# A linear-attention block in front of two MLPs on one core: the stretch ahead of the first MLP step rebuilt, and the first steps and attention levels put in another order

## The chip, the core and the metric

The kernel runs on one core of a Trainium2 chip. Five engines work side by side: TensorE multiplies matrices into PSUM (PE in the profile, its weight loads PEld), VectorE (DVE), ScalarE (ACT) and GpSimd (POOL) work on tiles, and SyncE (SP) issues most DMAs. Each engine takes its instructions in the order in which they are written; they wait for each other on semaphores. The metric is device time in microseconds of one launch.

## What is computed

The attention runs over 24 chunks of 32 tokens for 4 batches and 8 heads; its output, as 3072 tokens of 256 values, goes through a squared-relu MLP and then through a second MLP with a clipped gate. Cut to its core:

```python
for c in range(nc):
    cum = np.cumsum(la, axis=-1)                       # la: log of the decays of this chunk
    L = np.exp(cum[:, :, :, None] - cum[:, :, None, :]) * causal
    y_intra = np.einsum('bhij,bhjd->bhid', np.einsum('bhin,bhjn->bhij', Cc, Bc) * L, xc)
    y_inter = np.einsum('bhin,bhnd->bhid', Cc, state) * np.exp(cum)[:, :, :, None]
    y[:, :, sl] = y_intra + y_inter
    Bx = np.einsum('bhjn,bhjd->bhjnd', Bc, xc) * np.exp(cum[:, :, -1:] - cum)[:, :, :, None, None]
    state = np.exp(np.sum(la, axis=-1))[:, :, None, None] * state + np.sum(Bx, axis=2)

x = x.transpose(0, 2, 1, 3).reshape(3072, 256)
h = np.maximum(x @ w_in, 0.0);  x = (h * h) @ w_out    # first MLP, 256 -> 2048 -> 256
h = x @ w2_in;  y = (h * np.clip(h + 3.0, 0.0, 6.0) / 6.0) @ w2_out
```

## The kernel before

**Attention by levels.** The kernel takes chunks of 64 tokens (`CH`); the same chunk of all four batches is one *level*, so there are 12 levels, 0 to 11. Two levels make a tile of 512 tokens for the MLP: tile t needs levels 2t and 2t+1. For a level, `load`, `load_ef` and `load_x` bring B, C, the decays and x; `scale` multiplies the decays `ef` into B and C (tile `bc`), `heads` writes C masked by head (`cb`), `tokens` multiplies decays into the token-wise B (in tile `xb`), `scores` multiplies B by masked C on TensorE, `mask` copies the causal part to `mt`, `inter`, `intra` and `update` are the three products of the level, `advance` makes the next state S, and `evac_h` (ACT) and `evac_l` (DVE) split the output into a high and a low part (`act_h`, `act_l`).

**The decays.** `products` scans the decays of all chunks on 96 rows; `decays` makes the scaled products and inverses (`efr`) on DVE for four chunks, two at a time; `spread` brings them by TensorE to the 128 rows of levels 0 and 1, `f_tokens` transposes them for `tokens`; levels 2 to 11 read them back from DRAM (`scr`), which `decays_out` writes.

**The first MLP by steps.** A step (t, f) takes one tile t and one block f of 128 of the 2048 hidden columns. `mm1` makes six matmuls of 512 columns (`ha`), `gate` is relu and square on ACT (or the square on DVE) and a split of the result into `gha` (ACT) and `gla` (DVE), and `mm2` makes six matmuls (`ya`) for the step two before it (`LAG` 2). There are 96 steps. The list `ORDER` says in which order they come: ten blocks of tile 0, ten of tile 1, the last six of tile 0, the last six of tile 1, then tile after tile. The sum of a tile that is interrupted is kept in `part`.

**The weights.** The first MLP's weights come in 16 pieces j of 512 KB (even j for `mm1`, odd for `mm2`; pieces 2q and 2q+1 serve blocks 2q and 2q+1). Each is loaded raw (`dma`), converted on ACT (`early`), rebuilt on DVE by three instructions (`join`: `sign`, `bits`, `merge`) and split into `ah` on ACT and `al` on POOL (`split`). `JOIN1` and `DMA1` say at which step a piece is joined and loaded.

**What sets the order.** There is no scheduler: the order in the program is the order on each engine. `PLAN` says which attention work is put at which step; from level 2 on a level takes four steps. In a step, attention work of TensorE (`state`: `inter` and `update`; `chunk`: `intra` and the next level's `scores`) comes behind `mm1`; the rest comes in `mid`, behind the gate, and `advance` there comes last, behind the `join`. A new step's split of a weight is made by `ready`, between the relu and the square. `keep_busy` issues bf16 matmuls on zeros that fill TensorE's idle time ahead of the first step. SP's DMAs rotate over eight semaphores; the ninth is issued when the first has landed. Pools of PSUM: `ps_s` (tile `big`, later `yu`) and `ps_a` (tile `att`, one buffer) have four banks each; a new `att` tile waits for the last reader of the old one.

## Time and profile before

| | us |
|---|---|
| median of 3 runs | 582.83 (581.58 to 583.52) |
| the profiled execution, its own time | 582.18 |
| span of the profiled execution | 580.5 |
| TensorE busy | 559.0 (96%) |
| DVE, ACT, POOL busy | 414.6, 362.3, 143.6 |
| first `ha` matmul of the first step starts | 22.34 |

In the profile, times are counted from the span's start. A row of the timeline has the start, the duration, the engine, the line, the operation with its output and inputs, the number of instructions that the row merges, and in brackets the idle time of the engine before it with what ended it. Durations of merged rows are those of the whole stretch. The float32 matmuls of the attention stand twice in the trace for each one in the program. 1.68 us of the profiled execution's time lie outside its span.

### The profile page before, as it was taken

What the parts mean: (1) busy time and instruction counts of PE and PEld (TensorE: products, weight loads), DVE (VectorE), ACT (ScalarE), POOL (GpSimd) and SP (SyncE); (2) the same over time, 40 slices, a digit from 0 to 9 for tenths busy, and PEclk for the clock granted to TensorE, in tenths of its full rate; (3) what the DMA queues carried; (4) which work ended last, traced back from release to release, by engine and by line L of the source; (5) the groups of instructions that cost most, each with busy time, mean ns of one, the idle gap of its engine ahead of it and who ended that gap; (6) DMA issues with size and microseconds to landing.
All of it is one profiled execution on the core that took longest, in us unless ns stands there. A gap on an engine that the chain in (4) does not pass through costs nothing.

```text
span 580.5 us, 10441 instructions
## 1 busy us (share of the span) xinstructions
PE 559.0 (96%) x4144; PEld 446.8 (77%) x4144; DVE 414.6 (71%) x658; ACT 362.3 (62%) x632; POOL 143.6 (25%) x196
## 2 busy tenths in 40 slices
PE   7799989999999999999999899999999999999996
PEld 3476667777778888888887688888788888788885
DVE  5797577766655676676776876887767978676774
ACT  4577675544444656665665776777766777666663
POOL 4465334420000244434258300330000600000000
PEclk9789999999999999999999999999999999999999
DMA  8895244213000212212210000000200000200002
GB/s 246 224 259 137 63 125 132 81 51 102 2 1 0 72 41 71 70 43 69 74 40 34 1 1 0 1 1 1 73 1 0 1 1 1 73 1 0 1 0 73
DMA packets 26464, 31.42 MB, mean 54 GB/s; under 512 B 2128, under 2 KB 21040, under 8 KB 26416
## 3 DMA queue, kind: packets, MB, share of 16 engines
q1 hardware_dynamic: 24544, 29.85, 18.2%
q10 hardware_dynamic: 1872, 0.92, 0.6%
q8 instruction: 32, 0.52, 0.4%
q14 instruction: 16, 0.13, 0.1%
HBM read 27.41 MB, written 3.35 MB: 53 GB/s over the span
## 4 chain that ended last, share of the span: by engine, by line
PE 78%; DVE 6%; DMA 5%; ACT 3%; issue 3%; POOL 3%; SPq 1%; ACTq 0%; DVEq 0%; POOLq 0%
PE y L702 23%; PE ya L551 16%; PE ha L517 16%; PE X L657 11%; PE Z L657 6%; DMA ef<-scr 3%; PE V L657 3%; DMA rawa<-in_w1o 1%; PE att L347 1%; DVE ga L530 1%; ACT ga L524 1%; PE att L315 1%; POOL wtb L457 1%; DMA scr<-efr 1%; DVE mt L323 1%
## 5 line engine op out<-in xcount | busy, mean ns | idle before, releaser
L534 DVE TENSOR_TENSOR gla<-ga,gha 128x512 fp32r<-128x512 f32 x96 | 76.0, 793 | 37.4 <-ACT gha L532 37.0
L532 ACT ACTIVATE gha<-ga 128x512 fp32r<-128x512 f32 x96 | 60.6, 632 | 56.1 <-DVE ga L530 55.8
L524 ACT ACTIVATE ga<-ha 128x512 f32<-128x512 f32 x96 | 57.2, 596 | 55.9 <-PE ha L517 55.6
L530 DVE TENSOR_TENSOR ga<-ga,ha 128x512 f32<-128x512 f32 x81 | 55.4, 684 | 39.2 <-ACT ga L524 39.0
L517 PE MATMUL ha<-act_h,ah 128*128 128x512 f32 x192 | 75.9, 395 | 1.7 <-ACT act_h L387 1.2
L551 PE MATMUL ya<-gha,ah 128*128 128x512 f32 x192 | 77.1, 401 | 0.0
L551 PE MATMUL ya<-gla,ah 128*128 128x512 f32 x192 | 75.2, 392 | 1.4 <-DVE gla L534 1.4
L517 PE MATMUL ha<-act_h,al 128*128 128x512 f32 x192 | 75.6, 394 | 0.7 <-POOL al L477 0.7
L551 PE MATMUL ya<-gha,al 128*128 128x512 f32 x192 | 75.0, 391 | 0.0
L517 PE MATMUL ha<-act_l,ah 128*128 128x512 f32 x192 | 75.0, 391 | 0.1
L688 DVE TENSOR_TENSOR glc<-c,ghc 128x512 fp32r<-128x512 f32 x96 | 67.5, 706 | 5.9 <-ACT ghc L685 4.6
L679 DVE SCALAR_TENSOR_TENSOR c<-rc,c 128x512 f32<-128x512 f32 x72 | 51.0, 708 | 23.8 <-ACT rc L671 23.4
L671 ACT ACTIVATE rc<-c,three 128x512 f32<-128x512 f32 x72 | 52.0, 722 | 24.9 <-DVE c L666 24.7
L702 PE MATMUL y<-ghc,bh 128*128 128x512 f32 x168 | 65.5, 390 | 0.0
L702 PE MATMUL y<-glc,bh 128*128 128x512 f32 x168 | 65.4, 389 | 0.0
L702 PE MATMUL y<-ghc,bl 128*128 128x512 f32 x168 | 65.4, 389 | 0.0
L685 ACT ACTIVATE ghc<-c 128x512 fp32r<-128x512 f32 x96 | 58.6, 629 | 3.4 <-DVE c L679 3.2
L666 DVE TENSOR_TENSOR c<-Z,u 128x512 f32<-128x512 f32 x48 | 33.1, 690 | 22.9 <-PE Z L657 22.0
L517 PEld LDWEIGHTS ha<-act_h,ah 128*128 128x128 f32 x192 | 36.3, 189 | 11.0 <-ACT act_h L387 2.2
L551 PEld LDWEIGHTS ya<-gla,ah 128*128 128x128 f32 x192 | 36.0, 188 | 10.3 <-DVE gla L534 2.7
L662 ACT COPY u<-X 128x512 f32<-128x512 f32 x48 | 28.2, 588 | 24.3 <-PE X L657 24.3
L503 POOL TENSOR_TENSOR bl<-wtb,bh 128x256 fp32r<-128x256 f32 (+1 forms) x42 | 34.9, 865 | 34.2 <-ACT bh L496 29.8
(299 smaller groups left out, 1032.6 us busy)
## 6 DMA issues: line engine op xcount, KB each, us to landing
rawa<-in_w1i SPq DMA_DIRECT2D x8, 512.0 KB
rawa<-in_w1o SPq DMA_DIRECT2D x8, 512.0 KB
rawb<-in_w2i SPq DMA_DIRECT2D x8, 512.0 KB
rawb<-in_w2o SPq DMA_DIRECT2D x8, 512.0 KB
xb<-in_x SPq DMA_DIRECT2D x24, 128.0 KB
ef<-scr SPq DMA_DIRECT2D x10, 256.0 KB
out_yT<-xf SPq DMA_DIRECT2D x10, 256.0 KB
bc<-in_cT SPq DMA_DIRECT2D x6, 256.0 KB
```

Of the source, the lines that this page charges most:

```text
L517: nc.tensor.matmul(out=h, lhsT=wt[fb][:, k, fo * P:fo * P + P], rhs=xt[t][:, k, :], start=i == 0, stop=i == 5)
L524: nc.scalar.activation(out=g, in_=h, func=AF.Relu)
L530: nc.vector.tensor_tensor(out=g, in0=g, in1=h, op=ALU.mult)
L532: nc.scalar.activation(out=gh, in_=g, func=AF.Copy)
L534: nc.vector.tensor_tensor(out=gl, in0=g, in1=gh.bitcast(F32), op=ALU.subtract)
L551: nc.tensor.matmul(out=ys[m], lhsT=terms[i][0][fb][:, fo, m * P:m * P + P], rhs=terms[i][1], start=first and i == 0, stop=last and i == 2)
L657: nc.tensor.matmul(out=self.ps[bank], lhsT=lhsT, rhs=rhs, start=start and i == 0, stop=stop and i == 2, skip_group_check=True)
L671: nc.scalar.activation(out=self.sb["r" + c], in_=src, func=AF.Relu, bias=three)
L679: nc.vector.scalar_tensor_tensor(out=self.sb[c], in0=self.sb["r" + c], scalar=6.0, in1=src, op0=ALU.min, op1=ALU.mult)
L685: nc.scalar.activation(out=self.gh[c], in_=self.sb[c], func=AF.Copy)
L688: nc.vector.tensor_tensor(out=self.gl[c], in0=self.sb[c], in1=self.gh[c].bitcast(F32), op=ALU.subtract)
L702: nc.tensor.matmul(out=ys[t][m], lhsT=terms[i][0][:, 7 + 2 * (1 - f) + m], rhs=terms[i][1], start=first and i == 0, stop=last and i == 2, ...
```

## The change

- **Decays level by level.** `inverse` and `decays` make the decays of one chunk at a time: chunks 0 and 1 on DVE, 2 and 3 by scaled copies on ACT. `spread` runs once per level. `scaled_heads` makes the masked C of level 0 on DVE straight from PSUM; `gammas_first` moves to ACT. The zeroing of the two `mt` tiles moves from POOL to DVE and ACT.
- **Levels 0 and 1 one behind the other.** `scores(0)` comes ahead of everything for level 1, `scores(1)` behind `mask(0)`; the chain ends with `evac_h(1)`. There are 11, 3 and 3 matmuls of `keep_busy` in place of 13, 9, 2, 4 and 4.
- **Loads.** B and C of levels 2 and 3 (`load(2)`) and weight piece 2 come ahead of the decays' way through DRAM; weight piece 3 comes behind it. The token-wise B of level 1 is issued by ACT.
- **Weights ahead of the first step.** Pieces 0 and 2 are joined ahead of the first step, piece 1 in it.
- **Order of steps.** `ORDER` is eight blocks of tile 0, all of tile 1, the rest of tile 0, then tile after tile. Only tile 0 is interrupted.
- **Attention plan.** Levels 2 and 3 are planned by hand; from level 4 on a level takes five steps. `advance` follows `update` at once, `evac_h` follows `intra` and the next `scores` at once; the next level's `scores` at step 1 go into the tile that is there already. `ready` (a weight's split) comes ahead of the relu for tiles 0 to 2. `JOIN1`, `DMA1`, `SQUARE` follow.

The core of the diff:

```diff
-FIRST = 10
-ORDER = [(t, f) for fs in (range(FIRST), range(FIRST, NF)) for t in range(2) for f in fs]
+FIRST = 8
+ORDER = [(0, f) for f in range(FIRST)] + [(1, f) for f in range(NF)] + [(0, f) for f in range(FIRST, NF)]
...
-JOIN1 = {0: 3, 1: 4, 2: 5, 3: 6, 4: 7, 6: 8, 7: 9, 10: 10, 12: 11, 14: 12, 15: 13, 18: 14, 20: 15}
+JOIN1 = {0: 1, 1: 3, 2: 4, 3: 5, 4: 6, 6: 7, 9: 8, 10: 9, 12: 10, 13: 11, 15: 12, 17: 13, 18: 14, 20: 15}
...
+    def inverse(k, n):
+        i, o = divmod(k, 2)
+        nc.vector.reciprocal(out=ef5[i][:, o:o + n, 1, :], in_=prod.rearrange("p (c t) -> p c t", t=CH)[:, k:k + n])
+
+    def decays(k, scaled):
+        i, o = divmod(k, 2)
+        e = ef5[i][:, o]
+        scaled(e[:, 0, 0:SEG], p4[:, k, 0, :], e[:, 1, SEG - 1:SEG])
+        scaled(e[:, 1, 0:SEG], e[:, 1, 0:SEG], gs[:, 0, k:k + 1])
...
+    def scaled_heads(l):
+        d, f = lev[l], lev[l].pop("ef").rearrange("p b (w t) -> p b w t", w=2)
+        d["cb"] = at2.tile([P, 2, NB, CH], F32, tag="cb", name=f"cb{l}")
+        for e in range(2):
+            nc.vector.scalar_tensor_tensor(out=d["cb"][:, e], in0=f[:, :, 0], scalar=hm[:, e:e + 1], in1=d["bc"][:, :, 0, :],
+                                           op0=ALU.mult, op1=ALU.mult)
+        b = d["bc"][:, :, 1, :]
+        nc.vector.tensor_tensor(out=b, in0=f[:, :, 1], in1=b, op=ALU.mult)
...
     def from_state(l):
...
         update(l)
+        advance(l)
 
     def from_chunk(l):
...
             scores(l + 1, lev[l]["t"][:, :, 0:G])
+        evac_h(l)
...
+    spread(big, 0)
+    inverse(1, 1)
+    decays(1, by_vector)
+    scaled_heads(0)
+    sc = ps_a.tile([P, NPR, TOK], F32, tag="att", name="att_s")
+    spread(sc[:, :, G:], 1)
+    scale(1, nc.vector)
...
+    scores(0, big[:, :, 0:G])
+    mask(0, (0, 1))
+    heads(1)
...
     def first_scores(l):
-        sc = ps_a.tile([P, NPR, TOK], F32, tag="att", name=f"att_s{l}")
-        scores(l, sc[:, :, 0:G])
+        scores(l, lev[l - 1]["t"][:, :, 0:G])
```

DVE ahead of the first step, before: the decays of two chunks at a time (`efr`), both levels' scaling (`bc`), the first weight piece (`lowa`, `wta`), and behind it all four masks (`mt`).

```order
L183 RECIPROCAL efr<-prod 96x2x64
L184 COPY gs<-efr 96x2
L185 TENSOR_TENSOR efr<-efr,gs 96x2x32
L187 TENSOR_TENSOR efr<-prod,gs 96x2x32
L289 TENSOR_TENSOR bc_112<-big,bc_112 128x8x64 x2
L220 TENSOR_SCALAR gam_101<-big,hm 128x4x3 x2
L438 TENSOR_SCALAR lowa_246<-rawa_115 128x512
L443 TENSOR_SCALAR lowa_246<-rawa_115 128x512
L448 SCALAR_TENSOR_TENSOR wta_187<-wta_187,lowa_246 128x512
L323 COPY_PREDICATED mt_92<-tri,att_s 128x512 x2
L323 COPY_PREDICATED mt_93<-tri,att_s 128x512 x2
```

The same engine and place now.

```order
L180 RECIPROCAL efr<-prod 96x64
L190 TENSOR_SCALAR efr<-prod,efr 96x32
L190 TENSOR_SCALAR efr<-efr,gs 96x32
L301 SCALAR_TENSOR_TENSOR cb_185<-big,hm,bc_113 128x256 x2
L304 TENSOR_TENSOR bc_113<-big,bc_113 128x4x64
L294 TENSOR_TENSOR bc_113<-att_s,bc_113 128x8x64
L338 COPY_PREDICATED mt_92<-tri,big 128x512 x2
L180 RECIPROCAL efr<-prod 96x2x64
L455 TENSOR_SCALAR lowa_262<-rawa_116 128x512
L460 TENSOR_SCALAR lowa_262<-rawa_116 128x512
L465 SCALAR_TENSOR_TENSOR wta_233<-wta_233,lowa_262 128x512
```

The masks of level 0 stand ahead of the decays of chunks 2 and 3 and of the first weight piece; the masked C of level 0 is made here and not on ACT.

DVE in the first steps, before: the new state `S` of level 1 behind the joins of weight pieces 2 and 3.

```order
L448 SCALAR_TENSOR_TENSOR wta_422<-wta_422,lowa_429 128x512
L438 TENSOR_SCALAR lowa_478<-rawa_133 128x512
L443 TENSOR_SCALAR lowa_478<-rawa_133 128x512
L448 SCALAR_TENSOR_TENSOR wta_422<-wta_422,lowa_478 128x512
L372 TENSOR_TENSOR S_486<-att_361,S_353 128x256
L374 TENSOR_TENSOR S_486<-S_486,gam_101 128x256
L534 TENSOR_TENSOR gla_0_449<-ga_0_450,gha_0_448 128x512
```

The same engine and place now.

```order
L465 SCALAR_TENSOR_TENSOR wta_354<-wta_354,lowa_411 128x512
L387 TENSOR_TENSOR S_458<-att_314,S_342 128x256
L389 TENSOR_TENSOR S_458<-S_458,gam_101 128x256
L455 TENSOR_SCALAR lowa_465<-rawa_130 128x512
L460 TENSOR_SCALAR lowa_465<-rawa_130 128x512
L465 SCALAR_TENSOR_TENSOR wta_233<-wta_233,lowa_465 128x512
L551 TENSOR_TENSOR gla_0_438<-ga_0_439,gha_0_437 128x512
```

`S` stands ahead of the join of the step's weight piece (piece 1 here) and no longer behind a join.

SP behind the loads of levels 0 and 1, before: the decays' way through DRAM (`scr`, `ef`) ahead of B and C of levels 2 and 3 (`bc_216`).

```order
L423 DMA rawa_129<-in_w1o 128x1024
L423 DMA rawa_131<-in_w1i 128x1024
L423 DMA rawa_133<-in_w1o 128x1024
L226 DMA gsc<-gs 12x8x4 x2
L192 DMA scr<-efr 4x24x128 x4
L229 DMA gl<-gsc 128x1x96
L273 DMA ef_214<-scr 128x1x512
L255 DMA bc_216<-in_cT 128x4x128
L255 DMA bc_216<-in_bT 128x4x128
```

The same engine and place now.

```order
L440 DMA rawa_130<-in_w1o 128x1024
L260 DMA bc_132<-in_cT 128x4x128
L260 DMA bc_132<-in_bT 128x4x128
L440 DMA rawa_135<-in_w1i 128x1024
L231 DMA gsc<-gs 12x8x4 x2
L197 DMA scr<-efr 4x24x128 x4
L440 DMA rawa_241<-in_w1o 128x1024
L278 DMA ef_243<-scr 128x1x512
```

B and C now stand ahead of the decays' way through DRAM, and the first `ef` has the same transfers ahead of it as `bc_216<-in_bT` had, but for the 48 KB of `gl`.

## Rows read from the trace of the kernel before

**Rows 1.** Page, part 1: busy time, share of the span, instructions.

```profile
PE 559.0 (96%) x4144; PEld 446.8 (77%) x4144; DVE 414.6 (71%) x658; ACT 362.3 (62%) x632; POOL 143.6 (25%) x196
```

**Rows 2.** Windows: stretch, length, busy time per engine, granted clock, DMA share, GB/s.

```profile
22.30:28.95 6.65, 3.62 (x45) 2.42 (x45) 6.27 (x11) 5.32 (x11) 5.04 (x6) 1.00 1.03 269
28.95:62.47 33.52, 30.92 (x448) 23.02 (x448) 26.03 (x41) 24.89 (x50) 20.97 (x24) 0.95 0.70 183
62.47:90.00 27.53, 25.71 (x406) 19.80 (x407) 19.03 (x33) 18.43 (x34) 9.55 (x12) 1.00 0.42 118
```

**Rows 3.** Timeline of all engines ahead of the first step.

```profile
1.21 0.27 DVE L800 MEMSET seg<- 96x256 f32 x1
...
1.50 1.35 ACTq L265 DMA_DIRECT2D xb<-in_bK  x2
...
2.88 1.28 ACT L804 ACT_TABLE_LOAD   x1 [2.88 <-issue]
...
4.46 0.94 DVE L183 RECIPROCAL efr<-prod 96x128 f32<-96x128 f32 x1
...
6.85 1.99 PE L198 MATMUL big<-efr,sel 96*128 96x259 f32 x8 [0.74 <-DVE efr L187]
...
8.77 0.88 PE L208 MATMUL ftp<-ident,efr 96*64 96x96 f32 x16
8.88 1.29 DVE L289 TENSOR_TENSOR bc<-big,bc 128x512 f32<-128x512 f32 x2 [0.71 <-PE big L198]
...
9.58 2.12 PE L793 MATMUL ftp<-idle 128*128 128x512 bf16 x9
...
13.17 0.48 ACT L214 COPY ft<-ftp 64x96 f32<-64x96 f32 x2
...
14.21 0.67 ACT L434 ACTIVATE wta<-rawa 128x512 f32<-128x512 f32 x1
...
15.13 2.58 DVE L323 COPY_PREDICATED mt<-tri,att_s 128x512 f32<-128x512 uint32 x4 [3.06 <-POOL al L477]
...
18.51 0.42 DVE L374 TENSOR_TENSOR S<-yu,gam 128x256 f32<-128x256 f32 x1 [0.80 <-PE yu L793]
...
21.33 0.65 ACT L387 CAST act_h<-att 128x256 fp32r<-128x256 f32 x2 [1.72 <-PE att L347]
...
22.34 0.47 PE L517 MATMUL ha<-act_h,ah 128*128 128x512 f32 x1
```

**Rows 4.** Timeline of all engines, steps 0 to 2.

```profile
21.84 1.43 POOL L289 TENSOR_TENSOR bc<-ef,bc 128x256 f32<-128x256 f32 x2 [6.04 <-DMA bc<-in_bT]
...
25.57 0.39 PE L517 MATMUL ha<-act_l,ah 128*128 128x512 f32 x1
...
26.80 2.15 POOL L477 TENSOR_TENSOR al<-wta,ah 128x256 fp32r<-128x256 f32 x2 [0.32 <-ACT ah L475]
27.15 0.89 ACT L298 ACTIVATE cb<-bc,hm 128x256 f32<-128x256 f32 x2
...
28.28 0.41 DVE L372 TENSOR_TENSOR S<-att,S 128x256 f32<-128x256 f32 x1
...
28.95 1.16 PE L315 MATMUL att_s<-cb,bc 32*64 32x128 f32 x32 [2.98 <-POOL al L477]
```

**Rows 5.** Timeline, TensorE: three later places where it stood.

```profile
53.93 0.50 PE L517 MATMUL ha<-act_h,al 128*128 128x512 f32 x1 [0.73 <-POOL al L477]
...
62.47 0.50 PE L517 MATMUL ha<-act_h,ah 128*128 128x512 f32 x1 [1.19 <-ACT act_h L387]
...
86.74 0.86 PE L347 MATMUL att<-mt,xb 64*32 64x64 f32 x64 [1.76 <-DVE S L372]
```

**Rows 6.** Chain that ended last: start, duration, six matmuls in steady state.

```profile
91.16 1.36 PE ya L551 x6
```

**Rows 7.** One line's instructions: count, ns min/median/max, first and last start.

```profile
L448 DVE SCALAR_TENSOR_TENSOR wta<-wta,lowa x14: 691/692/1137, 11.4 to 85.7; 128x512 uint32<-128x512 uint32 x14
```

More of the change, by code (lines that the diff above doesn't have):

```diff
@@ new lines, in by_scalar, with decays_out, spread @@
+    def by_scalar(out, in_, f):
+        nc.scalar.activation(out=out, in_=in_, func=AF.Copy, scale=f)
+    def decays_out(i):
+        for k in (2 * i, 2 * i + 1):
+            nc.sync.dma_start(out=scr[k].rearrange("s h b w t -> b (s h) (w t)"), in_=ef[:, i, k % 2 * P:k % 2 * P + P])
+    def spread(efp, l):
+        n = P + l * (CPG - 1)
+        for b in range(NB):
+            nc.tensor.matmul(out=efp[:, b, 0:n], lhsT=sel[:, b], rhs=ef[:, 0, l * P:l * P + n], start=True, stop=True)
+        lev[l]["ef"] = efp[:, :, 0:P]
@@ L206, in f_tokens @@
+    def f_tokens(i, out):
+        ftp = out.rearrange("p (j r) -> p j r", j=2)
         for j in range(2):
@@ L542, in mm2 @@
         fb, fo = divmod(f, 2)
[L543 to L544 removed]
+        first = f == 0 or not t and f == FIRST
+        last = f == NF - 1 or not t and f == FIRST - 1
         if first:
@@ L826, in attn_mlp_mlp @@
     w1.dma(4)
+    gammas_in()
+    load_x(3)
     w1.dma(5)
[L828 to L854 removed]
+    w1.sign(0)
+    w1.bits(0)
+    place(0, ps_s.tile([P, 4, TOK], F32, tag="big", name="yu0"))
+    scores(1, lev[0]["t"][:, :, 0:G])
+    intra(0)
+    place(1, ps_a.tile([P, NPR, TOK], F32, tag="att", name="att1"))
+    lev[0]["u"] = lev[1]["u"]
+    evac_h(0)
+    w1.merge(0)
+    update(0)
+    f_tokens(1, lev[1]["t"][:, 1, 0:2 * R0])
+    keep_busy(3, lev[1]["t"][:, 3, 0:G], G)
+    advance(0)
+    mask(1, (0, 1))
+    f_tokens_out(1)
+    w1.early(1)
+    w1.split(0)
+    w1.early(2)
     inter(1)
     intra(1)
[L857 to L859 removed]
     evac_h(1)
+    evac_l(0)
     evac_l(1)
[L862 to L863 removed]
+    w1.sign(2)
+    w1.bits(2)
+    w1.merge(2)
+    tokens(1)
     scale(2)
[L865 to L867 removed]
     start_ctx.close()
```

158 lines of the change are left out of this document (58 added, 100 removed).

## Prediction

> **What bounds the kernel now.** I read the page first: TensorE is busy for 96% of the span [rows 1], so a gain can only come from places where it stands, or runs at half clock, or has not begun. Then the windows. From 62.47 us on TensorE is busy for 25.71 of 27.53 us at full clock; ahead of that, from 22.30 to 62.47, it has two poor stretches: 3.62 of 6.65 us, and 30.92 of 33.52 at a mean clock of 0.95 [rows 2]. The first useful `ha` matmul starts only at 22.34 [rows 3]. So three things are to be priced: when the first step starts, what the first ten steps lose, and what stands later. The timelines say what ends each wait.
>
> Six matmuls in steady state take 1.36 us [rows 6], a step of twelve 2.72. That work is the same before and after, so everything below is a difference in waiting.
>
> **The stretch ahead of the first step.** I follow the new order with the durations of rows 3, from the end of the scan, which is unchanged: the reciprocal at 4.46.
> - DVE: a reciprocal of half the columns takes half of 0.94, so 0.5, and two small scalings 0.2 each: done at 5.4. But the first `spread` also reads a copy of ACT. ACT issues two more DMAs (two took 1.35), so its table load, 1.28 long, starts at 4.2 and not at 2.88, and the copy is done near 5.9. The spread starts there and not at 6.85. It has 128 of 259 columns: half of 1.99, 1.0. Done at 6.9.
> - DVE then makes the masked C and the scaled B of level 0: three pieces of 256 columns out of PSUM, each like `S`, 0.42: 8.2. Level 1's scaling is half of 1.29: 8.85. The masks of level 0, half of 2.58: after `scores(0)` (0.6 on TensorE), 10.2. The double reciprocal, 0.94: 11.15.
> - ACT then scales chunks 2 and 3 in four pieces, each like half of the 0.48 copy: 0.24, so 12.1. TensorE meanwhile does `scores(1)`, `intra(0)` and `update(0)` (0.6, 0.9 and 0.5) from 10.2 to 12.3, then `f_tokens(1)`, half of 0.88, and three narrow fills (nine wide ones took 2.12, so 0.24 each): 13.5. `advance(0)` waits for the fills, as `S` at 18.51 did [rows 3]: 14.0.
> - Behind it: level 1's masks on DVE, 1.29, 15.3, and the rest of `intra(1)`, about 16.0. On ACT, which comes later: a copy 0.48, then three weight pieces at 0.67 at most: 16.5. Then `evac_h(1)`, 0.65: 17.15.
>
> TensorE's first `ha` came 0.36 after the end of `evac_h(1)` (21.33 plus 0.65, to 22.34) [rows 3]. So **the first step starts near 17.5**, 4.8 earlier.
>
> One edit is costed at nothing: the zeroing of 1024 columns moves to DVE. A memset of 256 columns took 0.27 [rows 3], so 1.07, in DVE's wait for `av`, which I put at 1.48 to 2.55 of a wait to 2.85; if that cover is gone, the chain moves by what sticks out. Beside work of POOL a DVE instruction can be much slower: `merge` takes 0.692 at the median and 1.137 at most [rows 7]. The Trainium skill ("SBUF — State Buffer", section "SBUF: two separate sides") says that VectorE and GpSimd share one pair of ports as an exclusive lock held for a whole instruction. By that rule the memset could stand behind POOL's own setup and the first step would come up to 0.5 later; the memset of 256 columns in rows 3 ran beside POOL's and shows nothing of it, so I take nothing.
>
> **Steps 0 and 1.** Before, TensorE finished step 1's `mm1` at 25.96 and stood 2.98 until `scores(2)` at 28.95 [rows 4]. The view names POOL, but what was late is the new `att` tile: `scores(2)` went into it, and it waited for the reader of the old one, `S` of level 1 at 28.28 plus 0.41, at the end of DVE's queue. Now the scores go into the old tile and `S` stands ahead of a join. What is late next is `cb` of level 2. It needs `scale(2)` on POOL (1.43), and that needs the first `ef`. Its place in SP's queue is that of `in_bT`, behind the same transfers, so it lands at the latest when POOL started before, 21.84 [rows 4], and, as the queue has 10 us of DMA share 1.0 ahead of it that don't depend on the decays, I take 20.5. So `scale(2)` ends at 21.9 and `cb`, 0.89, at 22.8. ACT's own queue gives the same: the join of piece 2 on DVE ends near 19.4, its split at 20.0, relu, square and copy of step 0 at 21.9. **`scores(2)` starts near 23.2, 5.75 earlier** (4.9 with 21.84; 6.5 without any wait).
>
> **From there to tile 1.** Before, `scores(2)` to the first matmul of tile 1 is 28.95 to 62.47, 33.5 us, of which two steps (5.4) now come behind the change of tile: 28.1 remains. Out of it fall three waits. Weight pieces 8 and 9 are no longer needed there: 1.1 in two waits, the second 0.73 [rows 5]. Tile 1's `act_h` was 1.19 late [rows 5]; now `evac_h(3)` comes at step 6, a whole step ahead. One small wait on `S`, 0.3. Together 2.6. In come two: weight piece 4 now has to be split within ACT's first four gates (a gate is three pieces of 0.6, and with five weight pieces and two `cb` ACT has 9 us of work behind 22.8; POOL's 2.15 for a split [rows 4] follows), 1.2; and `update(2)` behind `tokens(2)`, 0.4. The low part of level 3, behind a mask in DVE's queue, 0.5. The half clock after the wait at 28.95 (`scores(2)` took 1.16) stays in: the wait is about as long. Net 2.6 - 2.1 = **0.5 gained**.
>
> **Later.** At 86.74 TensorE stood 1.76 for `S` of a level that was queued behind a join [rows 5]. That order is gone: **1.76**. One interruption of a tile less saves copies that no row shows TensorE waiting for: nothing. Attention now ends at step 46 instead of 41, still ahead of its pools' closing at step 49: nothing. The weights from piece 8 on have three steps or more between split and use: nothing.
>
> Sum: 5.75 + 0.5 + 1.76 = **8.0 us**. The profiled execution's own 582.2 becomes 574.2; the median of the runs lies 0.65 above it, so **574.8**.
>
> **The rivals.**
> 1. *DVE sets the pace of the first eight steps.* It was busy 26.03 of 33.52 us [rows 2]; two joins and two low parts leave (8 pieces of 0.69) some 20.5 in 27.6, about the same share. But all of it is now packed against POOL's splits; if half of it ran at 1.137 instead of 0.692 [rows 7], it would take 27.2, and TensorE would lose some 4: 578.8. For it: DVE was busy 6.27 of 6.65 us at the start of the steps [rows 2]. Against: contention is in the old rows already.
> 2. *TensorE runs at half clock longer.* Fills fall from 32 to 17. Before, the clock was at 0.95 on average over the second window, with `scores(2)` at half clock behind a wait of 2.98 [rows 2, 4]. If it stays at 1.2 GHz from `scores(2)` to step 3's `mm1`, 5.9 us of work take twice that, less 1.7 that the sum holds already: +4.2, 579.0. Steps 0 and 1 at half clock cost nothing, since `cb` ends the wait behind them. The Trainium skill ("TensorE: Matmul & The Clock Gate", section "What's actually happening") says "the default state is throttled, and activity releases the throttle"; by that rule fewer fills speak for this rival. Against: the useful pieces stand closer now.
> 3. *Slower than before: DVE stands at `S`.* `advance` right behind `update` makes DVE wait for TensorE at each level, and everything behind it (a join, a mask, the low part of a gate) with it; then split, `al` and the next `mm1` are late. Priced at the one such wait on record, 1.76, for seven of the ten levels: 574.8 + 12.3 = 587. It decides against the change from five levels on. Against: `update` starts about 0.7 behind `mm1`, while ACT's relu takes 0.6 anyway.
> 4. *The change doesn't do what it says,* because transfers and not order set the pace: SP issues the second read of the decays behind ACT's scaling now. If `ef` for levels 2 and 3 landed 6 us later than I say, all but the late waits would be lost: 581.5.
>
> **How the numbers follow.** Chances: the forecast 0.62, reaching from 570 (no wait at `scores(2)`, none for piece 4) to 578 (hand-overs between engines, of 0.05 to 0.36, on top); rival 1 0.15, rival 2 0.09, rival 3 0.08, rival 4 0.06. The range from 570 to 580.5 leaves out rivals 3 and 4 and a little on the low side, under 0.2. What this measurement can tell from no change is about 0.3%, 1.75 us: faster is below 581.1. Faster: 0.61 + 0.14 + 0.08 + 0.01 = 0.84. Same: 0.01 + 0.01 + 0.01 + 0.05 = 0.08. Slower: 0.08.
>
> **What would show it.** First `ha` near 17.5; `scores(2)` near 23.2 with ACT's `cb` as what ended the wait; the first matmul of tile 1 (now step 8) near 50.8, without a wait for `act_h`; no wait of `intra` on `S` of more than 0.3. Rival 1 shows as long `merge` rows and waits on `al`; rival 2 as granted clock under 0.9 from 20 to 35; rival 3 as DVE idle ahead of `S`; rival 4 as POOL idle until `ef` beyond 24. A first `ha` later than 20 would make the whole sum wrong.

## The result, and the profile after

| | before | after |
|---|---|---|
| median of the runs side by side, us | 582.21 (581.12 to 583.52, 4 runs) | 575.02 (574.95 to 575.80, 4 runs) |
| the profiled execution, its own time | 582.18 | 575.03 |
| its span | 580.5 | 573.3 |
| first `ha` starts | 22.34 | 19.07 |
| the place from which the same work is left, called step 8 below | 57.01 (tile 1's first `ha` at 62.47, less the two steps of 2.73 that come later now) | 52.69 (tile 1's first `ha`) |
| from there to the end of the span | 523.5 | 520.6 |

The ratio is 0.9872, with a 95% interval of 0.985 to 0.9894: faster by 7.2 us, at 575.02 where 574.8 was forecast. Of the 7.2 us, 4.3 are gained by step 8 and 2.9 behind it.

Page of after, part 1 (it answers to [rows 1]):

```profile
PE 556.4 (97%) x4137; PEld 447.7 (78%) x4137; DVE 412.3 (72%) x655; ACT 366.3 (64%) x639; POOL 139.3 (24%) x194
```

Timeline of after, all engines, ahead of the first step (it answers to [rows 3]):

```profile
1.64 0.91 DVE L821 MEMSET mt<- 128x1024 f32 x1 [0.16 <-issue]
...
5.92 1.75 PE L203 MATMUL big<-efr,sel 96*128 96x128 f32 x8
...
14.77 0.42 DVE L389 TENSOR_TENSOR S<-att,gam 128x256 f32<-128x256 f32 x1 [0.80 <-PE att L813]
...
15.76 0.44 PE L349 MATMUL att<-bc,S 32*64 32x64 f32 x11 [1.02 <-ACT ft L220]
...
16.77 0.57 PE L349 MATMUL att<-bc,S 32*64 32x64 f32 x21 [0.57 <-issue]
...
17.27 1.06 PE L362 MATMUL att<-mt,xb 64*32 64x64 f32 x64
...
18.37 0.65 ACT L402 CAST act_h<-att 128x256 fp32r<-128x256 f32 x2 [0.88 <-PE att L362]
...
19.07 1.22 PE L534 MATMUL ha<-act_h,ah 128*128 128x512 f32 x2 [0.74 <-ACT act_h L402]
```

`S` comes at 14.77, and from there it is 4.3 us to the first `ha`. `inter(1)` (L349) stops after 11 of its 32 matmuls and goes on at 16.77; the bracket says `issue`, which is no engine. More on that below.

`spread(0)` took 1.75. One line's instructions, as in [rows 7], first of after, then of after_again, a second set of runs of the same program:

```profile
L203 PEld LDWEIGHTS big<-efr,sel x8: 192/333/334, 5.9 to 7.3; 96*128 96x128 f32 x8
L203 PEld LDWEIGHTS att_s<-efr,sel x8: 189/190/193, 7.4 to 8.2; 96*128 96x128 f32 x8
```

```profile
L203 PEld LDWEIGHTS big<-efr,sel x8: 187/192/192, 5.9 to 6.7; 96*128 96x128 f32 x8
```

The weight loads of `spread(0)` took 0.333 at the median, those of `spread(1)` right behind them 0.190. The loads of `mm1` take 0.33 in the stretch at half clock from 17.47 to 24.30 and 0.19 outside it, so `spread(0)` ran at half clock, until about 7.2. (The windows give 1.00 there, but the trace's record of the clock begins only at 7.23.) In after_again that record begins at 5.01, the loads took 0.192, `spread(0)` took 1.13, and `S` came at 14.16.

The first steps of after (it answers to [rows 4]):

```profile
21.73 1.42 POOL L294 TENSOR_TENSOR bc<-ef,bc 128x256 f32<-128x256 f32 x2 [2.73 <-DMA ef<-scr]
...
22.71 0.42 DVE L387 TENSOR_TENSOR S<-att,S 128x256 f32<-128x256 f32 x1 [1.35 <-PE att L376]
...
24.92 0.69 PE L330 MATMUL att<-cb,bc 32*64 32x128 f32 x32
...
28.17 0.98 DVE L465 SCALAR_TENSOR_TENSOR wta<-wta,lowa 128x512 uint32<-128x512 uint32 x1
...
29.08 1.34 DVE L338 COPY_PREDICATED mt<-tri,att 128x512 f32<-128x512 uint32 x2
...
30.52 0.69 PE L349 MATMUL att<-bc,S 32*64 32x64 f32 x32 [3.31 <-issue]
```

The wait of 2.98 at `scores(2)` in [rows 4] is gone: L330 has none. In its place TensorE stands 3.31 ahead of `inter(2)`. The row names nothing, but the mask of level 2 (L338) ends at 30.42, 0.10 ahead of it.

Windows of after (columns as in [rows 2]): two stretches at half clock, `scores(2)` to step 8, step 8 to the end, and 58 to 200 us.

```profile
17.47:24.30 6.83, 6.09 (x106) 4.37 (x89) 3.80 (x8) 3.50 (x9) 4.10 (x7) 0.50 0.83 250
31.12:34.53 3.41, 3.41 (x46) 2.64 (x40) 2.87 (x6) 2.43 (x6) 2.13 (x3) 0.50 1.12 293
24.92:52.69 27.77, 24.45 (x426) 18.89 (x425) 24.03 (x39) 21.36 (x41) 18.13 (x22) 0.94 0.85 219
52.69:573.30 520.61, 511.69 (x3365) 416.17 (x3363) 370.88 (x578) 331.70 (x567) 111.47 (x148) 1.00 0.13 38
58.00:200.00 142.00, 142.00 (x1686) 113.44 (x1687) 93.19 (x157) 81.54 (x150) 33.52 (x45) 1.00 0.24 69
```

The same stretches of the kernel before:

```profile
15.33:22.16 6.83, 6.17 (x181) 3.83 (x170) 4.50 (x10) 1.48 (x5) 0.79 (x2) 0.50 0.73 200
28.99:32.40 3.41, 3.41 (x38) 2.60 (x39) 3.27 (x6) 2.33 (x5) 2.06 (x3) 0.50 1.02 320
62.47:207.00 144.53, 142.38 (x1743) 112.97 (x1744) 92.98 (x157) 77.49 (x144) 30.96 (x41) 1.00 0.21 61
```

TensorE's idle time between 24.92 and 52.69 is 27.77 - 24.45 = 3.32 us, all of it the wait at `inter(2)`. From 58 to 200 it has none, where before it had 144.53 - 142.38 = 2.15. In these two executions the stretches at half clock ahead of step 8 last 6.83 and 3.41 us, 2.1 us later in the changed kernel. That is not fixed: in after_again the first one lasts 10.24, from 15.25 to 25.49.

### The profile page after: what moved, and what is told of

It is laid out like the page before. It is cut to its first block, busy times and chain, and to the rows that moved or that the text cites. A ratio compares the mean times of both kernels' runs of the same rounds, so it can differ in the third digit from the quotient of the medians.

```text
span 573.3 us, 10430 instructions
## 1 busy us (share of the span) xinstructions
PE 556.4 (97%) x4137; PEld 447.7 (78%) x4137; DVE 412.3 (72%) x655; ACT 366.3 (64%) x639; POOL 139.3 (24%) x194
## 4 chain that ended last, share of the span: by engine, by line
PE 89%; issue 3%; POOL 2%; DVE 2%; DMA 2%; ACT 2%; SPq 0%; DVEq 0%; POOLq 0%; ACTq 0%
PE y L722 23%; PE ha L534 21%; PE ya L568 21%; PE X L677 11%; PE Z L677 6%; PE V L677 3%; PE att L362 2%; PE att L349 1%; DMA rawa<-in_w1i 1%; PE att L330 1%; POOL wtb L474 1%; PE att L376 1%; POOL bl L520 1%; DMA rawa<-in_w1o 1%; POOL fb0t L617 1%
## 5 line engine op out<-in xcount | busy, mean ns | idle before, releaser
L551 DVE TENSOR_TENSOR gla<-ga,gha 128x512 fp32r<-128x512 f32 x96 | 74.5, 776 | 41.2 <-ACT gha L549 40.7
L682 ACT COPY u<-X 128x512 f32<-128x512 f32 x48 | 28.1, 586 | 24.4 <-PE X L677 24.4
L568 PEld LDWEIGHTS ya<-gha,ah 128*128 128x128 f32 x192 | 36.3, 189 | 9.4 <-issue 1.4
```

The source lines that it names most:

```text
L551: nc.vector.tensor_tensor(out=gl, in0=g, in1=gh.bitcast(F32), op=ALU.subtract)
L568: nc.tensor.matmul(out=ys[m], lhsT=terms[i][0][fb][:, fo, m * P:m * P + P], rhs=terms[i][1], start=first and i == 0, stop=last and i == 2)
```

## The experiments

Theory: the gain is the earlier start plus the waits that a better order on VectorE takes away, and what limits it now is VectorE's queue in the first steps. Rivals: the start is worth nothing behind a later wait; eight blocks of tile 0 instead of ten make the gain; the late waits went because of `advance`, or of the fifth step of a level.

All runs in one table. The profile is one execution of each kernel; the median is that of 4 to 6 timed ones, which lie up to 3.2 us apart. The sets of runs are from several chips; the kernel before gave 582.21 to 584.03 in them, and the changed kernel 575.02 in one and 575.88 in another. So the ratio to the kernel before on the same chip stands beside the median; its 95% interval is 0.0015 to 0.0032 to either side. Differences in the medians under 0.5 are not read, and between sets none under 0.9.

| run (chip) | first `ha` | step 8 begins | from there to the end | median, us | ratio to before |
|---|---|---|---|---|---|
| changed kernel | 19.07 | 52.69 | 520.6 | 575.02 | 0.9872 |
| the same again, after_again (1) | 19.30 | 53.79 | 520.6 | 575.88 | 0.9867 |
| old_start (13) | 22.23 | 54.27 | 520.6 | 576.59 | 0.9877 |
| first10 (13) | 19.42 | 53.82 | 520.8 | 575.69 | 0.9859 |
| mask2_early (13) | 18.13 | 54.15 | 520.7 | 574.58 | 0.9842 |
| adv_late (13) | 18.57 | 51.34 | 520.7 | 574.12 | 0.9833 |
| adv_late_mask2 (1) | 19.30 | 51.95 | 520.8 | 574.38 | 0.9837 |
| late1_mask2 (4) | 19.82 | 52.11 | 520.6 | 574.40 | 0.9853 |
| every4 (1) | 18.27 | 52.77 | 520.6 | 575.53 | 0.986 |
| every4_adv_late (1) | 19.44 | 52.23 | 520.7 | 574.38 | 0.9838 |
| every4_late_sq (4) | 18.29 | 52.23 | 521.7 | 575.99 | 0.989 |
| start2 (4) | 20.83 | 54.73 | 520.7 | 575.54 | 0.9875 |
| late_load (6) | 17.74 | 51.72 | 520.7 | 575.28 | 0.9857 |

Read the fourth column first: it is one number, 520.6 to 520.8, for every kernel but one. In the profiles, whatever was altered acted ahead of step 8.

> The changed kernel itself, unaltered, on the same chip and in the same rounds as the three below, so that differences of half a microsecond can be read. Every theory expects 575.0 within 0.5.

575.88 instead of 575.0: its wait at `inter(2)` was 3.29 and its step 8 came 1.1 us later. The 1.1 is there at `scores(2)` already, which started at 26.01, 0.10 behind `cb`: the `ef` that `scale(2)` waited for had landed by 23.36, and by 21.73 in the first profile. Two executions of one program differ that far here, so a difference of 1 us in a column of one profile needs a row that shows its cause.

### What the earlier start is worth

`old_start` puts the old stretch, from `Weights` to the closing of `ps_s`, in front of the new steps.

```diff
-    spread(big, 0)
-    inverse(1, 1)
...
+    decays(0)
...
-JOIN1 = {0: 1, 1: 3, 2: 4, ...
+JOIN1 = {1: 3, 2: 4, ...
```

> Undoes one part alone: the stretch ahead of the first step is that of the kernel before (both chunks' decays together, all masks together, 13, 9, 2, 4 and 4 fills, weight pieces 0 to 2 joined there), and the steps, the attention plan and the order of weights are those of the changed kernel.
> Theory A (the start's 3.3 us go through to the end one for one): first `ha` at 22.3, `scores(2)` near 28, tile 1's first matmul near 55.5, time 578.0 to 578.5.
> Theory B (the first steps wait for VectorE's queue, not for the first step, so an early start is partly used up in the wait at `inter(2)`; with piece 1 joined ahead of the steps that wait shrinks from 3.31 to under 1.5): first `ha` at 22.3 but time 575.5 to 577.
> If the start were worth nothing, 575.0.

Timeline of old_start, the places of `scores(2)` and `inter(2)` (its lines are numbered otherwise):

```profile
28.62 0.87 PE L325 MATMUL att<-cb,bc 32*64 32x128 f32 x32 [2.78 <-DMA xb<-in_bK]
...
32.80 0.69 PE L344 MATMUL att<-bc,S 32*64 32x64 f32 x32 [0.45 <-PE ha L529]
```

The first `ha` comes 3.16 later than in the changed kernel, `scores(2)` 3.70, `inter(2)` 2.28, and step 8 only 1.58 later. Theory B holds: with less in VectorE's queue the wait at `inter(2)` is 0.45 and not 3.31, and a good part of what the new start gains is taken back at that wait. (The row of `scores(2)` names a transfer, but `cb` ended 0.10 ahead of it.)

How much of the start reaches the end isn't settled: the median is 0.7 to 1.6 higher, the ratio by 0.0005 to 0.0010, which is 0.3 to 0.6 us and less than its interval. Seen from the other side it is clear: with the old start the new steps alone are 5.6 us below 582.21, and 7.1 below the kernel before on the same chip. Most of the gain doesn't need the new start.

### The wait at `inter(2)`

Four runs alter the order on VectorE alone. `mask2_early` puts the mask of level 2 ahead of the join of piece 3:

```diff
-PLAN = {0: ..., 1: ["first2", "tok2", "scale3", "~mask2"], ...
+PLAN = {0: ..., 1: ["first2", "tok2", "scale3", "mask2"], ...
```

> One edit: on VectorE the mask of level 2 comes ahead of the join of weight piece 3 and not behind it. In the changed kernel TensorE stands 3.31 us until `inter(2)` at 30.52; the mask's two instructions run from 29.08 to 30.42, the join ahead of them from 26.73 to 29.15.
> Theory A (the wait that `scores(2)` had for a new `att` tile has moved to `inter(2)`: the tile waits for the mask, the last reader of the old one): the mask now starts at 26.8 behind `gla` and ends at 28.2, `inter(2)` starts near 28.3, 2.2 us earlier, and TensorE stands about 1.1 there. Later stages have slack for the join, so the time falls by 1.5 to 2.5 us, to 572.5 to 573.5, with the interval's ratio near 0.984.
> Theory B (the profile writes `issue` and names no other engine: the wait is one for transfers or for POOL's `xb` and `bc`): `inter(2)` stays at 30.5 and the time stays at 575.0.
> Theory C (the join is as urgent as the mask): `inter(2)` moves to 28.3, but the weights of piece 3 come 1.3 us later and TensorE stands as long at the `mm2` that needs them, step 4; the time stays within 0.5 of 575.0.

Timeline of mask2_early, VectorE and TensorE:

```profile
26.49 1.36 DVE L338 COPY_PREDICATED mt<-tri,att 128x512 f32<-128x512 uint32 x2
27.95 0.69 PE L349 MATMUL att<-bc,S 32*64 32x64 f32 x32 [0.94 <-PE ha L534]
...
33.75 0.78 PE L362 MATMUL att<-mt,xb 64*32 64x64 f32 x55 [1.04 <-issue]
...
42.54 0.46 PE L349 MATMUL att<-bc,S 32*64 32x64 f32 x16 [1.33 <-issue]
...
49.31 0.69 PE L330 MATMUL att<-cb,bc 32*64 32x128 f32 x30 [1.84 <-issue]
```

The mask ends at 27.85 and `inter(2)` follows at 27.95. In the changed kernel it was 30.42 and 30.52, in adv_late 28.99 and 29.09: 0.10 behind the mask each time. So the wait is the one for the new `att` tile, whose last reader is now the mask. It shrinks from 3.31 to 0.94, as theory A said. The time falls by 0.4 to 1.3 in the medians, and the ratio is 0.9842, near the 0.984 of theory A. In the profiled execution (at 576.49 the slowest of its six) nothing is gained: TensorE stops three times in the middle of a row of like matmuls, 4.2 us together.

`adv_late` puts `advance` back behind the join:

```diff
     def first_update(l):
         update(l)
-        advance(l)
...
         decode(JOIN1, n)
...
+        for nm in PLAN.get(n, ()):
+            if nm.startswith(("state", "upd")) and int(nm.lstrip("staeupd")) < NLEV:
+                advance(int(nm.lstrip("staeupd")))
```

> Undoes one part alone: the instructions of `advance` (the new state S) stand again behind the weight's join of their step on VectorE, for every level, and not right behind `update`.
> Theory A (the 1.76 us that the prediction books for the later waits come from `advance` in its new place): the waits of `intra` on S come back, 1 to 2 us in all, time 576 to 577.
> Theory B (they come from the plan: with a level every fifth step, joins and `advance` fall into the same step at steps 2 and 9 only, and TensorE has nothing to wait for in the others): one wait of under 1 us at step 3, none from 62 us on, time 575.0 to 575.8.

Timeline of adv_late, the first steps:

```profile
27.63 1.36 DVE L338 COPY_PREDICATED mt<-tri,att 128x512 f32<-128x512 uint32 x2
...
29.09 0.69 PE L349 MATMUL att<-bc,S 32*64 32x64 f32 x32 [2.29 <-issue]
```

No late wait returns, which is theory B, and it is faster, by 0.9 in the medians and by 0.0034 or more in the ratio, which neither theory said. A pair on one chip agrees: every4_adv_late, which differs from every4 in this alone, gave 574.38 where every4 gave 575.53. In the changed kernel VectorE stood 1.35 for `update` ahead of `S` (22.71) with the join queued behind it; here the join comes first and `S` follows at 23.24 without a wait. The mask of level 2 comes 1.4 earlier; its first `ha`, 0.5 earlier, may be part of that.

`adv_late_mask2` has both edits, `late1_mask2` both with the late `advance` for level 1 alone.

> Two edits together: `advance` behind the join of its step (as in the run with that edit alone, which gave 574.1 and `inter(2)` at 29.09), and level 2's mask ahead of the join of piece 3 (alone: `inter(2)` at 27.95).
> Theory A (the wait at `inter(2)` is VectorE's queue and nothing else): the mask starts right behind `scores(2)`, `inter(2)` follows `mm1` of step 2 with under 0.4 of waiting, near 27.2, TensorE stays at full clock from there on, and the time is 572.0 to 573.0.
> Theory B (what the queue on VectorE gives, the fetch of TensorE's own instructions takes: in the run with the mask alone TensorE stood 1.04, 1.33 and 1.84 us in the middle of a row of equal matmuls, at 33.75, 42.54 and 49.31, with nothing in the row before it that it could wait for): `inter(2)` is early, but waits of 1 us and more appear inside groups of matmuls between 30 and 50, and the time is 573.8 to 575.

> Two edits on VectorE's queue in the first two steps only: `advance` of level 1 behind the join of piece 1 (all later ones stay right behind `update`), and level 2's mask ahead of the join of piece 3.
> Theory A (with every `advance` late TensorE stood 1.99 at 33.91 for S of level 2, which was queued behind a join; that wait goes, the one at `inter(2)` stays away, and nothing else is as late): `inter(2)` near 27.4, `intra(2)` without a wait over 0.5, time 0.5 to 1.5 below the run with both edits for every level, that is 573.0 to 573.9.
> Theory B (VectorE itself is the bound of the first eight steps, busy 24.4 of 27 us between 23 and 50, so a wait taken away here comes back at the next join, as one of `mm1` for a split weight or of `scores` for `cb`): the first matmul of step 8 stays within 0.5 of 51.95 and the time within 0.4 of 574.4.

Timeline of adv_late_mask2, steps 2 and 3:

```profile
27.46 0.69 PE L349 MATMUL att<-bc,S 32*64 32x64 f32 x32
...
33.91 0.86 PE L362 MATMUL att<-mt,xb 64*32 64x64 f32 x64 [1.99 <-DVE S L387]
```

The wait at `inter(2)` is gone, and TensorE keeps full clock from 23 to 50 us. But `intra(2)` now stands 1.99 for `S` behind two joins, and at 44.60 a split weight is 0.31 late. Neither theory holds: A expected 572 to 573, and B's time came without its stops inside rows of matmuls between 30 and 50. Late1_mask2 takes the 1.99 away and has 1.07 for `cb` and 0.57 and 0.31 for weights instead; its step 8 begins at 52.11, no earlier, though its first `ha` came 0.52 later. Its theory B fits: a wait taken away comes back at a later one, as VectorE is busy for 24.4 of 27 us there. All five times of adv_late_mask2 (573.63 to 574.66) lie below all four of the changed kernel on the same chip (574.99 to 576.80): against the kernel before it has a ratio of 0.9837 (0.9811 to 0.9862), the changed kernel there 0.9867 (0.984 to 0.9893).

### Eight or ten blocks of tile 0

```diff
-FIRST = 8
+FIRST = 10
...
-JOIN1 = {0: 1, 1: 3, 2: 4, 3: 5, 4: 6, 6: 7, 9: 8, 10: 9, 12: 10, ...
+JOIN1 = {0: 1, 1: 3, 2: 4, 3: 5, 4: 6, 5: 7, 6: 8, 7: 9, 12: 10, ...
```

> Undoes one part alone: ten blocks of tile 0 stand ahead of tile 1, as before, and not eight; weight pieces 7, 8 and 9 are joined at steps 5, 6 and 7 and pieces 8 and 9 loaded at steps 2 and 3.
> Theory A (the prediction's step: eight blocks take away the waits for pieces 8 and 9, 1.1 us before, because POOL and ScalarE split a piece per step): TensorE stands 0.7 to 1.5 us in all at steps 8 and 9, and time is 575.7 to 576.8.
> Theory B (the splits have caught up by then, since the level in between takes five steps and not four): no wait at steps 8 and 9, time 575.0 within 0.3.
> An `act_h` wait at the change of tile would be seen in neither.

TensorE is busy for all of 36 to 60.5 us: no wait for pieces 8 and 9, none for `act_h`. From step 4 to step 10 it takes 20.47 us, the changed kernel 20.48. What it loses, 1.1 us in the profile, it loses between `inter(2)`, which starts at 30.48 (30.52 in the changed kernel), and `intra(2)` at 37.13 (35.99). A window of first10 shows why, beside the window from 31.12 to 34.53 above:

```profile
29.74:36.57 6.83, 6.09 (x74) 4.88 (x75) 5.81 (x11) 4.33 (x10) 4.16 (x7) 0.50 1.08 289
```

Behind `inter(2)` it is at half clock for 6.1 us, the changed kernel for 3.4. The number of blocks is worth nothing here, as theory B said, though its time, 575.0 within 0.3, was missed.

### The late waits

`every4` and `every4_adv_late` restore a level every four steps, the second with late `advance` too; `every4_late_sq` then moves two squares to VectorE.

```diff
-        PLAN.setdefault(5 * _l - 10 + _k, []) ...
+        PLAN.setdefault(4 * _l - 6 + _k, []) ...
...
-SQUARE = (0, 1, 2, 3, 4, 5, 6, 7, 9, 10, 12, 13, 15, 17, 18, 20)
+SQUARE = (0, 1, 2, 3, 4, 5, 6, 7, 9, 10, 12, 15, 18, 20)
```

> Undoes one part alone: from level 4 on a level takes four steps again and not five; `advance` stays right behind `update`.
> Theory A (the later gain comes from `advance`'s place and the order within a level; the fifth step gives nothing): TensorE is busy without a gap from 50 us on as now, time within 0.4 of the changed kernel.
> Theory B (the fifth step is what took the late waits away, since it keeps a level's VectorE work out of the steps with joins): `intra` waits for S or `scores` for POOL's `bc`, 1 to 2 us in all, time 0.8 to 2.5 above the changed kernel.

> Undoes two parts: a level every four steps and `advance` behind the join, which together are the order of the kernel before from level 4 on. `state` then falls into steps 9, 13 and 17, which all have a join.
> Theory A (either of the two alone is enough to take the late waits away): waits of `intra` on S come back here alone, some 0.5 to 1.8 us each at up to three places (steps 10, 14, 18), time 1 to 3 above the run with a level every four steps alone.
> Theory B (the waits came from neither): no wait from 50 us on, and the time is that of the run with late `advance` alone.

> As the run with a level every four steps and late `advance`, which had no late wait, but the squares of steps 13 and 17 are VectorE's and not ScalarE's. Both steps have a weight's join and a level's `state`. In the kernel before, step 15 was such a step: its square (83.14), join (83.74 to 86.35) and S (86.27) stood one behind the other on VectorE, and TensorE stood 1.76 for S at 86.74.
> Theory A (that wait came from the three together, and went because the changed list of squares keeps VectorE's square out of every step with a join): at step 14 or 18 `intra` waits 0.5 to 1.8 us for S, and the time is 0.5 to 2.5 above 574.4.
> Theory B (it was something else, such as a transfer that came late): no wait from 50 us on, time 574.4 within 0.4.

The first two have no gap from 50 us on, so the late waits stay away without the fifth step and without the early `advance`. The third, timeline of VectorE and TensorE at steps 13 and 17:

```profile
71.97 0.69 DVE L546 TENSOR_TENSOR ga<-ga,ha 128x512 f32<-128x512 f32 x1 [1.00 <-ACT ga L540]
72.57 0.68 DVE L454 TENSOR_SCALAR lowa<-rawa 128x512 uint32<-128x512 uint32 x1
...
74.40 0.42 DVE L387 TENSOR_TENSOR S<-att,S 128x256 f32<-128x256 f32 x1
...
74.87 0.86 PE L362 MATMUL att<-mt,xb 64*32 64x64 f32 x64 [0.62 <-DVE S L387]
...
89.02 0.86 PE L362 MATMUL att<-mt,xb 64*32 64x64 f32 x64 [0.29 <-DVE S L387]
```

A square, a join and `S` stand one behind the other on VectorE, and waits like that of [rows 5] are back, 0.62 and 0.29. With 1.0 us more from step 8 to the end it is the one kernel whose fourth column differs; its median is 1.6 above that of every4_adv_late, from another chip. The wait is shorter than the 1.76 of before, where two instructions of the join at step 15 took 0.98 and 0.87 instead of 0.42 and 0.47: 0.96 of that wait.

In the kernel before, step 15 was such a step (join and `state`, but not in the list of squares); the changed list names every step that has a join. So the list of squares is enough to take the late waits away: theory A. It is not shown to be the only edit that does. With a level every five steps `state` comes at steps 9, 14, 19 and so on, and of these only 9 has a join, which the old list names too. By the plan the fifth step would then have been enough with the old list; no run tests that, nor the early `advance` with the old list.

### TensorE without instructions

`start2` rearranges the start:

```diff
-    f_tokens(1, lev[1]["t"][:, 1, 0:2 * R0])
-    keep_busy(3, lev[1]["t"][:, 3, 0:G], G)
     advance(0)
     mask(1, (0, 1))
-    f_tokens_out(1)
+    inter(1)
+    f_tokens(1, lev[1]["t"][:, 1, 0:2 * R0])
     w1.early(1)
     w1.split(0)
+    f_tokens_out(1)
     w1.early(2)
-    inter(1)
     intra(1)
```

> Three edits to the stretch ahead of the first step, none to the steps: ScalarE issues the token-wise B of level 1 behind the copies that `spread(0)` needs and not ahead of them; `advance(0)` and `inter(1)` come ahead of `f_tokens(1)`, which wrote the same tile as `inter(1)` and made it wait 1.02 us for ScalarE's copy; the three fills that S waited 0.80 for are left out, and ScalarE converts and splits the first weights ahead of that copy.
> Theory A (those are the terms by which the first step came 1.6 us later than forecast, besides the slower `spread`): spread(0) starts near 5.5 (5.92), S near 13.6 (14.77), `intra(1)` near 16 (17.27), first `ha` at 17.6 to 18.2 (19.07). The steps keep their wait at `inter(2)`, and about half of the gain reaches the end, as of the old start's 3.2 us half did: time 0.5 to 0.9 below the changed kernel on the same chip.
> Theory B (without the three fills TensorE falls to half clock earlier and takes back what the order gives): granted clock 0.5 from before 16 us on, first `ha` at 18.5 to 19.5, no change in time.

The output of this kernel is not the reference's (relative error 0.039), so it is no usable kernel, and only its times are read. That the transposes of `f_tokens(1)`, now behind `inter(1)` in a bank that holds part of its sums, are the reason wasn't tested. Timeline of start2, ahead of the first step:

```profile
13.55 0.42 DVE L389 TENSOR_TENSOR S<-att,gam 128x256 f32<-128x256 f32 x1
...
14.03 0.57 PE L349 MATMUL att<-bc,S 32*64 32x64 f32 x22 [1.00 <-DVE S L389]
...
16.91 0.58 PE L349 MATMUL att<-bc,S 32*64 32x64 f32 x10 [2.31 <-issue]
```

`S` comes 1.2 earlier, as theory A said (0.6 earlier than in after_again), and `inter(1)` starts 1.7 earlier. But it stops after 22 matmuls, and goes on at 16.91, where the changed kernel went on at 16.77. The first `ha` comes at 20.83, later than in either theory; the granted clock is 1.00 to 16.5 us, so theory B's reason is wrong as well.

Where TensorE stops is a place in its own instructions. Windows of start2 and mask2_early from 0 to just ahead of a stop (the counts behind x are TensorE's matmuls, then its weight loads):

```profile
0.00:16.50 16.50, 11.26 (x219) 6.84 (x221) 12.98 (x31) 8.00 (x21) 5.88 (x20) 1.00 0.79 222
```

```profile
0.00:33.50 33.50, 24.74 (x471) 15.88 (x472) 26.64 (x52) 19.90 (x44) 16.61 (x33) 0.95 0.85 239
0.00:42.40 42.40, 32.19 (x598) 21.69 (x599) 35.13 (x65) 26.60 (x58) 23.07 (x40) 0.96 0.85 229
0.00:49.20 49.20, 37.12 (x724) 25.37 (x726) 39.71 (x72) 31.48 (x67) 25.27 (x43) 0.97 0.87 227
```

440, 943, 1197 and 1450 records: the steps between them are 503, 254 and 253 (the 448 in the expectations counts the sequencer's own records too). Page of the changed kernel, part 3, queue, kind, packets, MB:

```profile
q8 instruction: 32, 0.52, 0.4%
```

That is 16 KB a packet, and TensorE's 8,274 matmuls and loads make 259 to a packet. The first of these packets ends at 15.38 in the changed kernel, 15.54 in start2 and 15.72 in late1_mask2, and TensorE goes on at 16.77, 16.91 and 17.05, 1.3 to 1.4 us later. In all, nine of the twelve profiles with the new start show TensorE going on at record 439 or 440, 1.31 to 1.43 us behind that packet's end, and the three stops of mask2_early end 1.44, 1.45 and 1.63 behind that of a later packet. So the stops are read as TensorE having run out of instructions; that the queue is TensorE's is inferred from these counts and times.

`late_load` tests whether the kernel's own loads hold that packet up. On top of late1_mask2:

```diff
     load(2)
-    w1.dma(2)
     constants()
...
     decays_out(1)
-    w1.dma(3)
+    w1.dma(2)
     load_ef(2)
     load_x(2)
     load_ef(3)
+    w1.dma(3)
...
-    w1.early(2)
     inter(1)
     intra(1)
     evac_h(1)
+    w1.early(2)
```

> On top of the two edits to VectorE's queue (late `advance` of level 1, early mask of level 2; 574.4): weight piece 2's load, 512 KB, goes behind the decays' way out to DRAM, piece 3's behind the first reads back, and the conversion of piece 2 behind `evac_h(1)`. Reason: in every run so far TensorE took up work again 1.3 to 1.4 us after the end of a 16 KB packet of the instruction queue (15.38 and 16.77 in the changed kernel, 15.54 and 16.91 in the run with the rearranged start, 15.72 and 17.05 in the run with these two edits), after 448 matmul and weight-load records whatever they were; the first `ha` came at 18.1 to 18.6 where that packet ended by 14.9, and at 19.1 or later where it ended behind 15.2.
> Theory A (the packet queues behind the kernel's own loads: piece 2's packets are under way from 13.0 to 14.9): with them gone it ends by 14.5, TensorE doesn't stop in `inter(1)`, first `ha` near 18.2 to 18.6, and the read of the decays for level 2 lands 1 us earlier, so that `scores(2)` comes near 24; time 572.5 to 573.8.
> Theory B (the packet is asked for when TensorE has got so far, and its time has nothing to do with the loads): it ends at 14.9 to 15.7 again, the stop in `inter(1)` stays, first `ha` at 18.9 to 19.8, time 574.4 within 0.5.
> Piece 2 must not become late for `mm1` of step 2; if it does, TensorE waits there for its split and the time is above 574.4.

Timeline of late_load:

```profile
15.40 0.69 PE L349 MATMUL att<-bc,S 32*64 32x64 f32 x32 [1.02 <-ACT ft L220]
...
17.74 0.73 PE L534 MATMUL ha<-act_h,ah 128*128 128x512 f32 x2 [0.74 <-ACT act_h L402]
...
20.57 1.81 POOL L294 TENSOR_TENSOR bc<-ef,bc 128x256 f32<-128x256 f32 x2 [1.93 <-DMA ef<-scr]
...
23.83 1.16 PE L330 MATMUL att<-cb,bc 32*64 32x128 f32 x32 [2.46 <-ACT cb L313]
...
30.00 0.65 PE L376 MATMUL att<-xb 64*32 64x64 f32 x32 [1.90 <-POOL xb L319]
```

The packet ends at 14.05, `inter(1)` runs in one piece, and the first `ha` is the earliest of all, 17.74: theory A for the start. The time doesn't follow. `scores(2)` stands 2.46 for `cb`, half clock follows, `update(2)` stands 1.90 for POOL, and the median is 575.28. In every4 (14.14, first `ha` 18.27) and mask2_early (14.68, 18.13) the packet ended early too, and no load was moved there, so one run with it early is not proof that the moved load did it.

## Why the prediction was right, and where not

The time was right, 575.02 for 574.8, and so were three things that it said would be seen: an earlier start, the wait at `scores(2)` gone, no late waits. That it was right to 0.2 us is luck. The sum's terms 5.75, 0.5 and 1.76 measured 4.0, 0.3 and 2.9, so two errors of over 1 us cancelled in part: in spans 8.0 were forecast and 7.2 came. The profiled execution also lay at the median of its runs now, where 0.65 was added.

**The path is wrong at one place: the start is carried through to the end one for one.** 5.75 of the 8.0 us stand for it and the wait at `scores(2)`. Old_start shows that most of the gain is there without it (5.6 us), and that what the start gains at `scores(2)`, 3.70, has shrunk to 1.58 by step 8. In its place the new order of the steps gained: with the old start `scores(2)` came at 28.62, hardly earlier than before, and step 8 at 54.27 for 57.01.

**First step at 17.5; it was 19.07.** `spread(0)` was put at 1.0 and took 1.75 in the profiled execution, since it ran at half clock; in after_again it took 1.13 and `S` came at 14.16 for the 14.0 forecast. So halving it with its columns was right, and the term that failed there is the clock: it was taken as full from the start. Between `spread` and `S` smaller errors cancel: the masks of level 0 end 0.3 later than `spread` explains, ACT's scaling 1.0 later, and `S` starts right behind the fills, where 0.5 was put. Behind `S` the step that failed was "ACT, which comes later": ACT was ready and waited 0.88 for TensorE. `inter(1)` had first to wait for the copy of `f_tokens(1)`, which shares its tile (until 15.76), then for instructions (until 16.77), and `intra(1)` ran at half clock. In late_load, without that stop, the first `ha` came at 17.74. The edit costed at nothing, the memset on DVE, was right: 0.91 at 1.64, done ahead of `av`. POOL's own setup ran beside it (0.84 at 1.92), and neither stood. The rule of a shared pair of ports (the Trainium skill, "SBUF — State Buffer", section "SBUF: two separate sides") did not show there.

**`scores(2)` at 23.2 with `cb` last; it was 24.92.** The chain is right: in late_load, where the start came as forecast (and a weight load was moved out of `ef`'s way), `scale(2)` starts at 20.57 (20.5 was taken) and `scores(2)` waits for `cb` until 23.83. In the changed kernel `scale(2)` waited for `ef` until 21.73, and `mm1` of step 1, in part at half clock, ended 0.2 behind `cb`; in after_again `ef` held it until 23.36 and `cb` was last again. The size that failed is the landing of `ef`. (With `ef` at 21.84 the prediction's own chain gives 4.4 us earlier, and not its 4.9; 4.0 came.)

**0.5 from there to tile 1; it was 0.3, by other terms.** The step that failed is "Now the scores go into the old tile". True, but `inter(2)` then needs the new tile, and its wait is for level 2's mask: 3.31 that the sum doesn't hold. The 2.6 of old waits did go. The 2.1 of new ones did not come: there is no wait for piece 4, for `tokens(2)` or for the low part of level 3. That sums to 0.7 lost; TensorE's busy time was 1.0 less than before's. Some 0.6 of this is what a wait costs beyond its idle time. In [rows 5] 0.73 of waiting is booked, but that matmul starts 1.23 behind the one ahead of it, where 0.23 is usual: 1.00 lost. The four old waits took 3.36 by such starts for 2.60 booked, the new one 3.48 for 3.31. The rest stays open. Eight blocks, which were credited with 1.1, gave nothing (first10).

**Later 1.76; it was 2.9.** 2.15 of it is idle time that went. The prediction put it down to `advance`, which is not needed for it (adv_late); the list of squares is enough (every4_late_sq), and `SQUARE` is not priced in the prediction at all. Whether the fifth step would have been enough too is open, and so is the other 0.7, which is busy time.

**The rivals.** Rival 1, VectorE's pace: half true. From `scores(2)` to step 8 VectorE was busy for 24.03 us, where its working expected some 20.5, and its queue decides where the first eight steps stand. The order on it matters (adv_late, mask2_early), and so does contention: between `S` of level 1 and the mask of level 2 four instructions beside POOL took 0.94, 0.95, 0.87 and 0.98, where their like take 0.42, 0.42, 0.47 and 0.69, 1.74 more in all ahead of a wait of 3.31. Rival 2, the clock: its 4.2 us did not come. That activity releases the throttle (the Trainium skill, "TensorE: Matmul & The Clock Gate", section "What's actually happening") spoke for it; in the two profiled executions the stretches ahead of step 8 add up to 10.2 us with 17 fills as with 32. But the clock did take its part: at `spread(0)`, and in after_again and first10, where these stretches add up to 13.7 us. Rival 3 is real, but at three levels out of ten: DVE stood 1.35, 0.36 and 1.11 at `S` of levels 1, 2 and 4, and the last cost TensorE nothing. Rival 4: `ef` was the last thing that `scale(2)` waited for, 1.2 later than taken and 2.9 in after_again, not 6. (Its price should be 581.1 and not 581.5: 574.8 and the 6.25 lost.)
